# Two loads on ScalarE's queue, PSUM banks that stay open, and an intermediate that moves into another tile

## The chip, the cores and the metric

The kernel runs on one core of a Trainium2 chip. The metric is the device time of one execution in microseconds (us); the median of several runs counts. The engines are called PE (TensorE, matmuls), DVE (VectorE), ACT (ScalarE), POOL (GpSimd) and SP (SyncE, which here only issues DMAs). SBUF is the on-chip working memory, PSUM the accumulator memory, of which the kernel uses eight banks of 128 x 512 fp32.

## The reference

Three layers in a row. First, attention with a window: 2 batches x 8 heads, 768 positions, head size 64; a query sees the 128 latest keys and 4 "sink" keys at the start. Then a dense layer with a smooth activation, then a mixture of four experts with ReLU:

```python
scores = np.where(is_sink | in_window, scale * q @ k.T, -1e9)
x = softmax(scores) @ v                  # 1536 tokens x 512
h = x @ w_in                             # 512 -> 2048, w_in and w_out in float64
x = (h * np.tanh(softplus(h))) @ w_out   # "mish", 2048 -> 512
p = domain_probs / (domain_probs.sum(-1, keepdims=True) + 1e-09)
out = sum(p[:, e:e + 1] * (np.maximum(x @ w1[e], 0) @ w2[e]) for e in range(4))  # 512 -> 1024 -> 512
```

## The kernel before, in words

Every big product is made of three matmuls on split numbers: each operand is a high part (`xh`, `wih`, `gh`) and a low part (`xl`, `wil`, `gl`), and high x high, low x high and high x low are added in PSUM.

Attention is cut into 24 *items* of 256 queries and two heads (`attention_item`). An item's data is one `qk` tile (`load_item`, L129 to L135) and one `v` tile (`attention_values`, L204 to L212); both DMAs are issued from SP's queue. Items are loaded two ahead (`AHEAD`). Items 0 and 1 have their `qk` loaded ahead of the program's branch on a flag; their `v`, and all of items 2 and 3, are loaded behind it. The scores go from PE into PSUM (`sc`, L231), DVE takes mask and row minimum (L234), ACT the exponential (L238), PE transposes (L264) and multiplies by `v` (L277), and ACT and DVE write the result as `xh` and `xl` (L184, L185).

The dense layer and the experts are cut into *units* of 512 hidden columns: units 0 to 3 are the dense layer, 4 to 11 the experts. A unit's weights come in pieces. In the dense layer each piece is float64 and is taken apart by ACT (L116) and DVE (L117 to L124). The pieces of unit 0 and, written back to DRAM ("parked"), of unit 1 and half of unit 2 are converted during attention.

`Experts.stream` gives the dense work in *steps*. Unit 0 is run in four chunks of tokens, here A (0 to 255), B (256 to 511), C (512 to 1023) and D (1024 to 1535). A chunk has four hidden blocks (`layer1`: 12 matmuls into one `h` bank, then `mish`) and four output blocks (`layer2`: 12 matmuls into one `o` bank, from the `gh` and `gl` of all four hidden blocks). The order is: block 1, block 2, output 1 of the chunk before, block 3, output 2, block 4, outputs 3 and 4. While attention runs, one step follows each item from the sixth item on, 19 steps in all: all of A and B's hidden blocks, A's outputs, all four blocks of C and B's outputs 1 to 3. What comes behind is traced after the attention's pools are closed.

PSUM during attention: one `h` bank and one `o` bank, three for `sc`, two for the transposes, one for `pv`. Behind attention these pools are closed, and new ones are opened: two banks for the intermediate `r`, three for `h`, three for `o`. During attention `r` is one SBUF tile instead. `mish` (L549 to L556, then the split at L89 and L97) has five ACT instructions on tiles `w`, `u`, `r`, three on DVE, then ACT writes `gh` and POOL writes `gl`. `w` and `u` have two buffers, `gh` and `gl` seven.

The order of instructions on each engine is set when the program is built: the framework's planner takes the written order, moves an instruction forward where by its modelled times it is ready, and adds the semaphore waits. On the chip each engine then runs its queue strictly in that order.

Of the kernel before, what the change touches and what calls it, by code (L numbers as in the profile page):

```python
# [9 lines left out]
F32 = mybir.dt.float32  # L10
# [3 lines left out]
AF = mybir.ActivationFunctionType  # L14
ALU = mybir.AluOpType
PSUM = bass.MemoryType.PSUM

P = 128
BIG = 8.0e9
C2, C1, C0 = 0.4889076793633006, -0.9463237919407588, -0.8989585617169157  # L20
# [5 lines left out]
QW = 2 * P  # L26
# [99 lines left out]
        nc.sync.dma_start(out=park, in_=lo.bitcast(F32))  # L126


def load_item(c, b, hp, i, pool=None):  # L129

    w = c.KW[min(i, 1)]
    raw = c.stage.next() if pool is None else pool.tile([P, QW + c.KW[1]], F32, tag="qk", name="qk")
    off = c.OFF[i]
    c.nc.sync.dma_start(out=raw[:, 0:QW + w], in_=c.qk[b, hp, :, off:off + QW + w])
    return raw  # L135


# [63 lines left out]
    return a  # L201


def attention_values(c, a, b, hp, i):  # L204

    v = a.v.next()
    n0 = 0 if i else 1
    c.nc.sync.dma_start(
        out=v[:, n0:3],
        in_=c.v[b, hp, (2 * i - 1 + n0) * P:(2 * i + 2) * P, :].rearrange("(n p) d -> p n d", p=P),  # L210
    )
    return v  # L212
# [165 lines left out]
class Experts:  # L378
# [5 lines left out]
    def __init__(self, c, ctx):  # L384
        self.c = c
        self.NF = self.FU // P
        self.KT = c.DM // P
        tp = c.tc.tile_pool
        self.acc = c.acc
        self.wpool = [ctx.enter_context(tp(name="m_w0", bufs=1)), None]  # L390
        self.cv = ctx.enter_context(tp(name="m_cv", bufs=1))
        self.tp = ctx.enter_context(tp(name="m_t", bufs=2))
        self.gp = ctx.enter_context(tp(name="m_g", bufs=7))
        self.units = []
        for u in range(c.F1 // self.FU):
            cols = slice(2 * u * self.FU, 2 * (u + 1) * self.FU)
            self.units.append((0, u, c.w_in[:, cols], c.w_out[u * self.FU:(u + 1) * self.FU, :]))
        self.n1 = len(self.units)
        for e in range(c.E):
            for u in range(c.F2 // self.FU):  # L400
                cols = slice(u * self.FU, (u + 1) * self.FU)
                self.units.append((1, e, c.w1[e, :, cols], c.w2[e, cols, :]))
        self.w = {}
        self.parked = {}

    def psum(self, ctx, nh, no, nr=0):
        tp = self.c.tc.tile_pool
        self.pr = ctx.enter_context(tp(name="m_pr", bufs=nr or 1, **(dict(space=PSUM) if nr else {})))
        self.pa = ctx.enter_context(tp(name="m_pa", bufs=nh, space=PSUM))
        self.pb = ctx.enter_context(tp(name="m_pb", bufs=no, space=PSUM))  # L410

    def park(self, pool, n, nm):

# [51 lines left out]
    def layer1(self, n, t0, cw, g):  # L465
        c, nc = self.c, self.c.nc
        kind, e, _, _ = self.units[n]
        NF, KT, n1 = self.NF, self.KT, self.n1
        x = (c.xh, c.xl)
        cols = slice(t0, t0 + cw)  # L470
        wis = self.w[n][0]
        for f in range(NF):
            h = self.pa.tile([P, self.CW], F32, tag="h", name="h")[:, 0:cw]
            fs = slice(f * P, (f + 1) * P)
            for k in range(KT):
                for t, (sw, sx) in enumerate(TERMS):
                    nc.tensor.matmul(  # L477
                        h, lhsT=wis[sw][:, k, fs], rhs=x[sx][:, k, cols],
                        start=k == 0 and t == 0, stop=k == KT - 1 and t == 2,
                    )  # L480
            gh = self.gp.tile([P, self.CW], F32R, tag="gh", name="gh")[:, 0:cw]
            gl = self.gp.tile([P, self.CW], F32R, tag="gl", name="gl")[:, 0:cw]
            if kind == 0:
                self.mish(n, gh, gl, h)
            else:
                nc.scalar.activation(gh, h, AF.Relu)  # L486
                nc.vector.scalar_tensor_tensor(gl, h, 0.0, gh.bitcast(F32), ALU.max, ALU.subtract)  # L487
            g.append((gh, gl))
            yield

    def layer2(self, n, t0, cw, g):
        c, nc = self.c, self.c.nc
        kind, e, _, _ = self.units[n]
        NF, KT, n1 = self.NF, self.KT, self.n1
        cols = slice(t0, t0 + cw)
        wos = self.w[n][1]
        if kind == 0:
            accv = self.acc.rearrange("p (ch d) w -> p ch d w", d=KT)
            for d in range(KT):
                o = self.pb.tile([P, cw], F32, tag="o", name="o")  # L500
                ds = slice(d * P, (d + 1) * P)
                for f in range(NF):
                    for t, (sw, sx) in enumerate(TERMS):
                        nc.tensor.matmul(  # L504
                            o, lhsT=wos[sw][:, f, ds], rhs=g[f][sx],
                            start=f == 0 and t == 0, stop=f == NF - 1 and t == 2,
                        )
                y = accv[:, t0 // c.DM, d, t0 % c.DM:t0 % c.DM + cw]
                if n == 0:
                    nc.scalar.activation(y, o, AF.Copy)  # L510
                else:
                    nc.vector.tensor_tensor(y, y, o, ALU.add)
                if n == n1 - 1:
                    split(c, c.xh[:, d, cols], c.xl[:, d, cols], y, nc.scalar, nc.vector)
                yield
            return
        last = n == len(self.units) - 1
        for d in range(cw // P):
            tt = t0 // P + d
            pcol = c.pn[:, tt, e:e + 1]  # L520
            ds = slice(d * P, (d + 1) * P)
            nw = 2 if last and tt == c.T // P - 1 else 1
            for q in range(nw):
                ms = slice(q * c.DM // nw, (q + 1) * c.DM // nw)
                o = self.pb.tile([P, c.DM], F32, tag="o", name="o")[:, ms]
                for f in range(NF):
                    for t, (sw, sx) in enumerate(TERMS):
                        nc.tensor.matmul(  # L528
                            o, lhsT=g[f][sx][:, ds], rhs=wos[sw][:, f, ms],
                            start=f == 0 and t == 0, stop=f == NF - 1 and t == 2,  # L530
                        )
                y = self.acc[:, tt, ms]
                if n == n1:
                    nc.scalar.activation(y, o, AF.Copy, scale=pcol)
                else:
                    nc.vector.scalar_tensor_tensor(y, o, pcol, y, ALU.mult, ALU.add)  # L536
                if last:
                    nc.sync.dma_start(out=c.out[tt * P:(tt + 1) * P, ms], in_=y)
            yield

    def mish(self, n, gh, gl, h):

        c, nc = self.c, self.c.nc
        cw = h.shape[-1]
        w, u = (self.tp.tile([P, self.CW], F32, tag=t, name=t)[:, 0:cw] for t in ("w", "u"))
        r = self.pr.tile([P, self.CW], F32, tag="r", name="r")[:, 0:cw]
        nc.scalar.activation(w, h, AF.Tanh, scale=0.5)  # L549
        nc.scalar.activation(w, w, AF.Square, scale=-0.5, bias=0.5)  # L550
        nc.scalar.activation(u, w, AF.Square, scale=C2, bias=C1)
        nc.scalar.activation(r, u, AF.Exp, bias=C0)  # L552
        nc.vector.scalar_tensor_tensor(u, w, 1.0, r, ALU.add, ALU.mult)  # L553
        nc.scalar.activation(u, u, AF.Square, scale=ROOT2, bias=-1.5 * ROOT2)
        nc.vector.scalar_tensor_tensor(u, u, 1.5, r, ALU.add, ALU.mult)
        nc.vector.scalar_tensor_tensor(w, u, 1.0, h, ALU.subtract, ALU.mult)  # L556
        split(c, gh, gl, w, nc.scalar, nc.gpsimd)
# [10 lines left out]
def banded(c, ctx, raws):  # L568
# [3 lines left out]
    first = ExitStack()  # L572
    x = Experts(c, ctx)
    w = x.weights(0)
    x.psum(first, 1, 1)
    a = attention_pools(c, first)
    steps = x.stream([(0, 0, QW), (0, QW, QW)] + [(0, t0, x.CW) for t0 in range(2 * QW, c.T, x.CW)] + later(c, x, 1))
    dram = ctx.enter_context(tc.tile_pool(name="park", bufs=1, space=bass.MemoryType.DRAM))
# [1 line left out]
    items = c.items  # L580
    raws = dict(enumerate(raws))
    preps = {}
    done = 0
    for m, it in enumerate(items):
        while done <= min(m + AHEAD, len(items) - 1):
            raw = raws.pop(done) if done in raws else load_item(c, *items[done], pool=a.qk)
            preps[done] = raw, attention_values(c, a, *items[done])
            done += 1
        attention_item(c, a, *it, preps.pop(m))
        if m < 4 or m in PARK:  # L590
            run(w, 1)
        if m >= LAG:
            run(steps, 1)
        if m == 0:
            normalize_probs(c)
    first.close()
    x.wpool[1] = ctx.enter_context(tc.tile_pool(name="m_w1", bufs=1))
    x.psum(ctx, 3, 3, 2)
    run(x.weights(1))
    run(steps, 4 * (x.NF + 4) - 4 - (len(items) - LAG))  # L600
    rest(c, x, steps, 1)
# [140 lines left out]
```

## Time and profile before

| what | before |
| --- | --- |
| median of 3 runs | 935.59 us (931.53, 935.59, 936.59) |
| the profiled execution: its own time | 931.33 us |
| span of its instructions | 929.5 us |
| PE busy | 905.6 us, 97% of the span |
| DVE, ACT, POOL busy | 424.6, 347.7, 263.7 us |
| mean granted clock of PE | 0.988 of full speed |

The busy times are sums over the span. The profile's page also cuts the span into 40 slices; there DVE is at 9 tenths in slices 2 to 6 and at 1 or 2 tenths in the second half. A "row" below is a line of an answer of the trace: start in us, duration, engine, line of the kernel, operation, and in brackets how long the engine sat idle before and what ended that.

### The profile page before, as it was taken

How to read it: one execution, taken by the hardware profiler on the slowest of the kernel's cores; microseconds unless marked ns; L12 is line 12 of the kernel's file. 1: busy time of each engine (PE TensorE's matmuls, PEld its weight loads, DVE VectorE, ACT ScalarE, POOL GpSimd, SP SyncE). 2: the span in 40 equal slices, each digit the busy share in tenths (PEclk: the TensorE clock that was granted, in tenths of full speed). 3: DMA queues.
4: the chain of work that ended last, by engine and by line, in shares of the span. 5: the costliest groups of instructions: out<-in, count | busy, mean ns of one | idle time of the engine just before them, and what ended most of it. 6: DMA issues, size and time to landing. Idle time of an engine off the chain costs nothing.

```text
span 929.5 us, 11138 instructions
## 1 busy us (share of the span) xinstructions
PE 905.6 (97%) x4292; PEld 730.6 (79%) x4292; DVE 424.6 (46%) x770; ACT 347.7 (37%) x745; POOL 263.7 (28%) x217
## 2 busy tenths in 40 slices
PE   6999999799999999999999999999999999999997
PEld 4566767688888888888888888888888888888886
DVE  6999995247698555641112222222222222222222
ACT  4788875487767767722221111111111111111110
POOL 4586663122222434520220220221122112200000
PEclk8999999989999999999999999999999999999999
DMA  7757752062123011001110110110110010000012
GB/s 234 249 189 242 251 215 80 17 255 91 46 90 136 1 46 46 23 23 46 46 40 7 45 46 1 46 46 0 46 46 24 23 45 1 1 1 1 11 46 83
DMA packets 33790, 67.03 MB, mean 72 GB/s; under 512 B 4144, under 2 KB 12592, under 8 KB 33728
## 3 DMA queue, kind: packets, MB, share of 16 engines
q1 hardware_dynamic: 33728, 66.23, 21.1%
q8 instruction: 36, 0.59, 0.3%
q14 instruction: 26, 0.21, 0.1%
HBM read 51.54 MB, written 9.44 MB: 66 GB/s over the span
## 4 chain that ended last, share of the span: by engine, by line
PE 86%; DVE 10%; ACT 1%; DMA 1%; issue 0%; POOL 0%; DVEq 0%; ACTq 0%
PE h L477 42%; PE o L528 28%; PE o L504 14%; DVE pr L234 2%; DVE cv_h L119 1%; DVE cv_a L123 1%; PE pv L277 1%; DVE cv_a L117 1%; DVE cv_r L122 1%; DMA stage<-in_moe_w_in_dram 1%; PE sc L231 1%; PE tp L264 1%; DVE cv_a L121 1%; DVE xl L185 1%; DVE cv_a L118 0%
## 5 line engine op out<-in xcount | busy, mean ns | idle before, releaser
L477 PE MATMUL h<-xh,wih 128*128 128x512 f32 (+1 forms) x592 | 229.2, 387 | 0.3 <-DVE w L556 0.3
L477 PE MATMUL h<-xh,wil 128*128 128x512 f32 (+1 forms) x592 | 227.8, 385 | 0.0
L477 PE MATMUL h<-xl,wih 128*128 128x512 f32 (+1 forms) x592 | 226.8, 385 | 0.0
L486 ACT ACTIVATE gh<-h 128x512 fp32r<-128x512 f32 x96 | 57.4, 598 | 410.1 <-PE h L477 245.2
L487 DVE SCALAR_TENSOR_TENSOR gl<-h,gh 128x512 fp32r<-128x512 f32 x96 | 66.4, 691 | 208.1 <-ACT gh L486 207.9
L528 PE MATMUL o<-wol,gh 128*128 128x512 f32 (+1 forms) x388 | 150.1, 387 | 0.0
L528 PE MATMUL o<-woh,gh 128*128 128x512 f32 (+1 forms) x388 | 150.1, 387 | 0.0
L528 PE MATMUL o<-woh,gl 128*128 128x512 f32 (+1 forms) x388 | 149.9, 387 | 0.0
L536 DVE SCALAR_TENSOR_TENSOR acc<-o,pn,acc 128x512 f32<-128x512 f32 (+1 forms) x85 | 63.3, 745 | 176.2 <-PE o L528 176.2
L477 PEld LDWEIGHTS h<-xh,wih 128*128 128x128 f32 x592 | 111.8, 189 | 24.5 <-DVE cv_a L117 0.7
L477 PEld LDWEIGHTS h<-xl,wih 128*128 128x128 f32 x592 | 111.5, 189 | 22.6 <-issue 0.5
L477 PEld LDWEIGHTS h<-xh,wil 128*128 128x128 f32 x592 | 111.7, 189 | 22.3 <-DVE wil L124 0.3
L97 POOL TENSOR_TENSOR gl<-w,gh 128x512 fp32r<-128x512 f32 (+1 forms) x52 | 68.2, 1312 | 168.0 <-ACT gh L89 167.8
L504 PE MATMUL o<-gh,woh 128*128 128x512 f32 (+1 forms) x208 | 79.4, 382 | 5.4 <-ACT gh L89 5.4
L528 PEld LDWEIGHTS o<-wol,gh 128*128 128x128 f32 x388 | 72.9, 188 | 14.9
L528 PEld LDWEIGHTS o<-woh,gh 128*128 128x128 f32 x388 | 72.9, 188 | 14.9
L528 PEld LDWEIGHTS o<-woh,gl 128*128 128x128 f32 x388 | 72.8, 188 | 14.7
L504 PE MATMUL o<-gh,wol 128*128 128x512 f32 (+1 forms) x208 | 78.2, 376 | 0.0
L504 PE MATMUL o<-gl,woh 128*128 128x512 f32 (+1 forms) x208 | 77.4, 379 | 0.0
L87 POOL TENSOR_SCALAR wih<-stage 128x1024 fp32r<-128x1024 f32 x16 | 16.5, 1048 | 189.4 <-PE h L477 189.4
L553 DVE SCALAR_TENSOR_TENSOR u<-w,r 128x512 f32<-128x512 f32 (+1 forms) x52 | 34.4, 662 | 50.2 <-ACT r L552 49.9
L87 POOL TENSOR_SCALAR woh<-stage 128x1024 fp32r<-128x1024 f32 x16 | 16.5, 1048 | 141.0 <-PE o L528 122.2
(84 smaller groups left out, 1101.5 us busy)
## 6 DMA issues: line engine op xcount, KB each, us to landing
stage<-in_moe_w_dram SPq DMA_DIRECT2D x32, 512.0 KB, 3.7
stage<-in_moe_w_in_dram SPq DMA_DIRECT2D x8, 1024.0 KB, 6.6
stage<-in_moe_w_out_dram SPq DMA_DIRECT2D x8, 1024.0 KB, 5.0
qk<-in_qk_dram SPq DMA_DIRECT2D x16, 324.0 KB, 5.4
acc<-in_v_dram SPq DMA_DIRECT2D x16, 192.0 KB, 3.6
woh<-cv_h SPq DMA_DIRECT2D x6, 512.0 KB, 2.9
out_dram<-acc SPq DMA_DIRECT2D x11, 256.0 KB, 2.0
wih<-cv_h SPq DMA_DIRECT2D x4, 512.0 KB, 3.0
```

The source lines that it names most:

```text
L87: eng.tensor_scalar(out, src, 1.0, 0.0, ALU.mult, ALU.add)
L97: eng_lo.tensor_tensor(lo, src, hi.bitcast(F32), ALU.subtract)
L117: nc.vector.tensor_scalar(af, af, TINY_HI, HUGE_HI, ALU.max, ALU.min)
L119: nc.vector.scalar_tensor_tensor(h, w_hi, -0x40000000, a, ALU.bitwise_and, ALU.bitwise_or)
L234: nc.vector.tensor_tensor_reduce(out=o, in0=sc, in1=c.masks[t if i == 0 else 2][:, 0:sw], scale=-c.scale, scalar=3.0e38, op0=ALU.add, op1= ...
L477: nc.tensor.matmul(h, lhsT=wis[sw][:, k, fs], rhs=x[sx][:, k, cols], start=k == 0 and t == 0, stop=k == KT - 1 and t == 2,)
L486: nc.scalar.activation(gh, h, AF.Relu)
L487: nc.vector.scalar_tensor_tensor(gl, h, 0.0, gh.bitcast(F32), ALU.max, ALU.subtract)
L504: nc.tensor.matmul(o, lhsT=wos[sw][:, f, ds], rhs=g[f][sx], start=f == 0 and t == 0, stop=f == NF - 1 and t == 2,)
L528: nc.tensor.matmul(o, lhsT=g[f][sx][:, ds], rhs=wos[sw][:, f, ms], start=f == 0 and t == 0, stop=f == NF - 1 and t == 2,)
L536: nc.vector.scalar_tensor_tensor(y, o, pcol, y, ALU.mult, ALU.add)
L553: nc.vector.scalar_tensor_tensor(u, w, 1.0, r, ALU.add, ALU.mult)
```

## The change

Three edits. (1) The `qk` and `v` loads of items 2 and 3 are issued from ACT's queue instead of SP's. (2) The `h` bank and the `o` bank of the attention stage are no longer closed with it; behind attention two more of each are opened and taken in rotation with the old one, instead of three new ones of each. (3) In the attention stage the intermediate `r` of `mish` is written into the `gl` tile of the same block, whose final content overwrites it at the end; the SBUF tile for it is gone.

```diff
-def load_item(c, b, hp, i, pool=None):
+def load_item(c, b, hp, i, pool=None, eng=None):
-    c.nc.sync.dma_start(out=raw[:, 0:QW + w], in_=c.qk[b, hp, :, off:off + QW + w])
+    (eng or c.nc.sync).dma_start(out=raw[:, 0:QW + w], in_=c.qk[b, hp, :, off:off + QW + w])
...
-def attention_values(c, a, b, hp, i):
+def attention_values(c, a, b, hp, i, eng=None):
-    c.nc.sync.dma_start(
+    (eng or c.nc.sync).dma_start(
...
     def psum(self, ctx, nh, no, nr=0):
         tp = self.c.tc.tile_pool
-        self.pr = ctx.enter_context(tp(name="m_pr", bufs=nr or 1, **(dict(space=PSUM) if nr else {})))
-        self.pa = ctx.enter_context(tp(name="m_pa", bufs=nh, space=PSUM))
-        self.pb = ctx.enter_context(tp(name="m_pb", bufs=no, space=PSUM))
+        k = len(self.banks)
+        if nr:
+            self.pr = ctx.enter_context(tp(name="m_pr", bufs=nr, space=PSUM))
+        for nm, n in (("h", nh), ("o", no)):
+            pool = ctx.enter_context(tp(name=f"m_p{nm}{k}", bufs=n, space=PSUM))
+            self.banks.setdefault(nm, []).extend([pool] * n)
+
+    def bank(self, nm):
+        pools = self.banks[nm]
+        pools.append(pools.pop(0))
+        return pools[-1].tile([P, self.CW], F32, tag=nm, name=nm)
...
-            h = self.pa.tile([P, self.CW], F32, tag="h", name="h")[:, 0:cw]
+            h = self.bank("h")[:, 0:cw]
...
-        r = self.pr.tile([P, self.CW], F32, tag="r", name="r")[:, 0:cw]
+        rr, r = gl, gl.bitcast(F32)
+        if self.pr:
+            rr = r = self.pr.tile([P, self.CW], F32, tag="r", name="r")[:, 0:cw]
-        nc.scalar.activation(r, u, AF.Exp, bias=C0)
+        nc.scalar.activation(rr, u, AF.Exp, bias=C0)
...
-    x.psum(first, 1, 1)
+    x.psum(ctx, 1, 1)
...
-            raw = raws.pop(done) if done in raws else load_item(c, *items[done], pool=a.qk)
-            preps[done] = raw, attention_values(c, a, *items[done])
+            eng = c.nc.scalar if done in (2, 3) else None
+            raw = raws.pop(done) if done in raws else load_item(c, *items[done], pool=a.qk, eng=eng)
+            preps[done] = raw, attention_values(c, a, *items[done], eng=eng)
...
-    x.psum(ctx, 3, 3, 2)
+    x.psum(ctx, 2, 2, 2)
```

The three places that took an `o` tile take `self.bank("o")` in the same way.

## Rows read from the trace of the kernel before

**Rows 1.** Page, head: busy us of each engine.

```profile
PE 905.6 (97%) x4292; PEld 730.6 (79%) x4292; DVE 424.6 (46%) x770; ACT 347.7 (37%) x745; POOL 263.7 (28%) x217
```

**Rows 2.** Stages: start:end, length, busy us (count) by engine, granted clock, DMA share, GB/s.

```profile
12.00:18.00 6.00, 2.75 (x14) 1.73 (x13) 2.46 (x12) 2.80 (x8) 2.85 (x5) 0.91 1.00 341
16.30:136.00 119.70, 112.75 (x734) 76.22 (x734) 116.76 (x308) 96.89 (x301) 78.18 (x82) 0.96 0.70 237
136.00:178.60 42.60, 42.50 (x241) 33.79 (x242) 18.80 (x34) 21.99 (x51) 12.03 (x11) 0.96 0.17 62
178.60:184.78 6.18, 0.83 (x4) 0.37 (x3) 2.07 (x3) 3.87 (x8) 0.00 (x0) 0.95 0.03 6
184.78:191.00 6.22, 6.22 (x15) 4.87 (x16) 2.64 (x4) 5.40 (x11) 2.57 (x2) 0.50 0.97 317
191.00:922.00 731.00, 731.00 (x3228) 605.31 (x3227) 273.58 (x380) 214.48 (x360) 163.14 (x103) 1.00 0.12 42
```

**Rows 3.** Timeline of the start: PE, ACT and DVE.

```profile
8.81 0.40 ACT L238 ACTIVATE pr<-pr,mx 128x128 f32<-128x128 f32 x1 [6.80 <-DVE mx L234]
...
16.30 1.12 ACT L116 ACTIVATE cv_a<-stage 128x1024 f32<-128x1024 f32 x1 [2.87 <-DMA stage<-in_moe_w_in_dram]
17.15 0.77 PE L231 MATMUL sc<-qk 64*128 64x128 f32 x2 [3.17 <-DMA qk<-in_qk_dram]
...
17.45 0.69 DVE L117 TENSOR_SCALAR cv_a<-cv_a 128x1024 f32<-128x1024 f32 x1 [2.62 <-ACT cv_a L116]
...
18.06 0.42 DVE L234 CUSTOM_DVE_ANT_0 pr<-sc,mask 128x256 f32<-128x256 f32 x1
...
20.48 0.28 DVE L234 CUSTOM_DVE_ANT_0 pr<-sc,mask 128x128 f32<-128x128 f32 x1
...
21.96 0.61 DVE L252 TENSOR_SCALAR pr<-pr,sm 128x128 f32<-128x128 f32 x2
```

**Rows 4.** Timeline of SP's DMA issues at the start.

```profile
8.20 0.39 SPq L134 DMA_DIRECT2D qk<-in_qk_dram  x1
8.70 0.37 SPq L208 DMA_DIRECT2D acc<-in_v_dram  x1
9.18 0.40 SPq L372 DMA_DIRECT2D stage<-in_moe_w_in_dram  x1
9.69 0.40 SPq L134 DMA_DIRECT2D qk<-in_qk_dram  x1
```

**Rows 5.** DMA issues of 0 to 30 us: count, KB each, median us to landing.

```profile
stage<-in_moe_w_in_dram SPq DMA_DIRECT2D x2, 1024.0 KB, 8.0
...
acc<-in_v_dram SPq DMA_DIRECT2D x4, 128.0 KB, 2.1
qk<-in_qk_dram SPq DMA_DIRECT2D x2, 256.0 KB, 5.2
```

**Rows 6.** Chain that ended last: start us, us, what (the load; then 163 to 200 us).

```profile
9.18 7.10 DMA stage<-in_moe_w_in_dram
...
163.41 4.98 PE h L477 x21
...
184.78 4.21 PE o L504 x9
...
196.84 2.72 PE h L477 x12
```

**Rows 7.** Timeline of ACT, DVE and PE behind attention.

```profile
162.84 0.69 DVE L556 SCALAR_TENSOR_TENSOR w<-u,h 128x512 f32<-128x512 f32 x1
...
177.49 1.09 ACT L549 ACTIVATE w<-h 128x512 f32<-128x512 f32 x2 [2.49 <-PE h L477]
...
179.50 1.15 ACT L551 ACTIVATE u<-w 128x512 f32<-128x512 f32 x2
...
183.38 0.69 DVE L556 SCALAR_TENSOR_TENSOR w<-u,h 128x512 f32<-128x512 f32 x1
...
184.63 0.58 ACT L552 ACTIVATE r<-u 128x512 f32<-128x512 f32 x1
184.78 0.79 PE L504 MATMUL o<-gh,woh 128*128 128x512 f32 x1 [5.35 <-ACT gh L89]
...
190.81 0.60 ACT L549 ACTIVATE w<-h 128x512 f32<-128x512 f32 x1
```

**Rows 8.** Waits of SP's own DMA queue, longest in total: us, times, longest.

```profile
SPq L434 <- DVE u L555: 35.2, 1, 35.2
```

More of the change, by code (lines that the diff above doesn't have):

```diff
@@ L403, in __init__ @@
         self.w = {}
+        self.banks, self.pr = {}, None
         self.parked = {}
@@ L499, in layer2 @@
             for d in range(KT):
-                o = self.pb.tile([P, cw], F32, tag="o", name="o")
+                o = self.bank("o")[:, 0:cw]
                 ds = slice(d * P, (d + 1) * P)
@@ L524, in layer2 @@
                 ms = slice(q * c.DM // nw, (q + 1) * c.DM // nw)
-                o = self.pb.tile([P, c.DM], F32, tag="o", name="o")[:, ms]
+                o = self.bank("o")[:, ms]
                 for f in range(NF):
```

## The prediction

> **What bounds the kernel now.** I read the engines' busy times first: PE works 905.6 us of the span and no other engine half of it [rows 1]. Then the stages [rows 2]. From 191 to 922 us PE is busy in all 731 us at full clock; the change adds and removes no matmul, so nothing is to be had there. From 16.3 to 136 us DVE is busy for 116.76 of 119.7 us: this stage ends when DVE has done its attention and weight conversions. From 136 to 178.6 PE has 42.50 of 42.60. What is left is three places: the start, up to 16.3 us; a hole in PE behind attention (178.6 to 184.78); and what follows that hole, 6.22 us at a granted clock of 0.50, which is the lower level, 1.2 GHz, after 5.35 us in which PE had nothing. Only 15 matmuls fit there; at full clock 12 take 2.72 us [rows 6], so 15 would take 3.40, and the low clock costs 2.8 us. Hole and low clock together are 8.2 us.
>
> At the start two things wait for DMAs [rows 3]: PE for the `qk` of item 3 (3.17 us, until 17.15), and ACT, with DVE behind it, for the first piece of `w_in` (until 16.30; DVE then starts at 17.45 after 2.62 us of nothing). SP's issues show why: the 1024 KB piece goes out at 9.18, item 3's `qk` behind it at 9.69 [rows 4, 5], and the piece takes 7.10 us [rows 6].
>
> In the hole, PE waits for ACT's `gh` of chunk C's block 4. All four blocks of C are traced inside attention, with its single `h` bank. So block 3 can only start when block 2's last reader (162.84 + 0.69 = 163.53) is done, block 4 when block 3's is, and the `gh` of block 4 comes at 184.7 [rows 7]. PE fills the time with blocks 1, 2 and 3 of chunk D, which have three fresh banks, until it has nothing left.
>
> **Part by part. (1) The loads.** Four issues leave SP (two `qk`, two `v`). SP's stand 0.5 us apart [rows 4], so the piece of `w_in` can go out at 8.20 instead of 9.18, 1.0 us sooner. On ACT no DMA issue appears in the trace; by SP's the four cost 4 x 0.5 = 2.0 us. ACT has nothing before 8.81 (6.80 us idle) [rows 3], so they run from about 7.2 to 9.2 and delay the first exponential by at most 0.4 us, which is hidden as long as DVE waits for `w_in` until 17.45. If the planner puts two of them between exponentials, it is 1.0 us and still inside that cover.
>
> Items 2 and 3 then travel beside the piece, not ahead of and behind it. Its end is pushed back by item 3's 256 + 128 KB; at the 341 GB/s of this stretch [rows 2] that is 1.15 us, against the 1.0 us of earlier issue. So the piece lands between 1.0 us sooner and 1.2 us later; I take 0.5 later. In exchange DVE can fill its 2.62 us hole: two 256-wide mask steps (0.42 each), two 128-wide (0.28) and a scaling pair (0.61) now stand behind L117 [rows 3], 2.0 us in all. So the start gains 2.0 - 0.5 = 1.5 us. Best: 2.0 + 1.0 = 3.0. Worst: the planner leaves that work behind L117 and the piece is late, a loss of 1.2. DVE has 3 us of slack in the next 120 us [rows 2], so I pass the 1.5 us on whole.
>
> The Trainium skill ("DMA: Bandwidth & Descriptors", section "Rules for kernel authors") speaks against this edit: spreading DMAs over several issuing engines adds no bandwidth, because they share the same 16 DMA engines and interleave, and only issue time is saved. The trace agrees that the DMA engines are full there (share 1.00 from 12 to 18 us); by that rule alone this part is worth zero or a small loss, which is the second rival.
>
> **(2) The banks.** Behind attention the rotation for `h` begins with the old bank. Chunk D's block 1 therefore gets the bank that block 4 of C holds until 183.38 + 0.69 = 184.07. Its 12 matmuls, which before were filler ahead of the hole, move behind it: 2.72 us of cover are lost. Two things come back. These 12 can start at 184.07, not at 184.78 with the `gh`: 0.71 us. And the filler had stood in the way: between 163.41 and 168.39 PE did 21 matmuls [rows 6], of which only 12 were block 3 of C; without D's block 1, blocks 3 and 4 of C come 0.7 us (3 of those 21) to 2.0 us (all 9) sooner; I take 1.3. Sum: 2.72 - 0.71 - 1.3 = 0.7 us lost. Best: the chain of C runs early enough to close the hole, 8.2 us gained. Worst: nothing sooner, and the 12 run wholly at the low clock (12 x 6.22 / 15 = 4.98), 4.98 - 0.71 = 4.3 lost. I stay at 0.7, since the single bank for C's four blocks, which makes the hole, is left as it is.
>
> The two PSUM banks of `r` no longer lie on the old `h` and `o` banks. Before, D's block 1 stood from 180.65 (end of L551) to 184.63 for one [rows 7]. That stall goes; it buys nothing on PE, which never waits again after 184.78. `o` has three banks before and after.
>
> **(3) `r` in `gl`.** ACT writes and DVE reads as many elements in SBUF as before, so the twelve blocks in question cost the same. `gl` is held from the exponential on, about 4 us longer, of seven buffers; since C's blocks wait for the `h` bank anyway, the seventh is not what comes last. Zero; at most one 0.6 us instruction either way. With the SBUF tile gone, the loads of unit 1's weights needn't wait 35.2 us for its last reader at 183.3 [rows 8]. They move into a stretch where the DMA share is 0.17 and later 0.03, off 184.78 to 191, where it is 0.97 [rows 2]. PE had no wait for them, so this is zero too.
>
> **Sum.** -1.5 + 0.7 = -0.8 us: the profiled execution would go from 931.33 to 930.5. The median of the runs lies 4.26 us above that execution, so on its scale it is 935.59 - 0.8 = 934.8 us. Such a step is less than a measurement of this kernel can tell: about 0.5%, 4.7 us.
>
> **Rivals.** *The hole closes* (faster). If the planner, with the stalls on `r` gone and fewer fillers at hand, puts C's blocks ahead of D's, the hole and the low clock behind it go: -8.2 - 1.5 = -9.7, 925.9 us. For it: block 3 stood 2.0 us behind foreign matmuls, and blocks 2 to 4 follow each other. Against: two full passes of `mish` at 6.6 us (177.49 to 184.07) stay in the chain, and half a hole may bring the low clock all the same.
>
> *The loads share the DMA engines* (no gain at the start): the piece lands 1.2 us later, DVE sits before L117 for that time, and the items gained early wait behind it in the queue. +1.2 + 0.7 = +1.9, 937.5 us. For it: DMA share 1.00. Against: DVE has ready work.
>
> *The kept bank starts a second hole* (slower). D's block 1 is done at 184.07 + 4.98 = 189.05, and its `mish` ends with the bank at 195.6 (6.6 later). PE's store from 184.07 on is 12 of block 1, 9 parts of C's outputs [rows 6] and C's output 4 (12): 33 matmuls, 15 in 6.22 and 18 in 4.08 us, to 194.4. Then 1.2 us of waiting for a bank. D's block 3 can take `w` and `u` only from block 1; before, they were held from the pair's second Tanh, at about 178.0, to 190.81 less the 4.0 of stall, 8.8 us, so its bank is free at 189.05 + 8.8 + 6.6 = 204.5, a second wait of about 1.1 us. If PE then drops to the low clock again, 2.8 more. 2.7 - 0.7 + 1.2 + 1.1 + 2.8 = +7.1, less the 1.5 of the start: +5.6, 941.2 us. It decides if D's blocks 2 and 3 do not get through `mish` while block 1 waits for its bank. For it: only two pairs of `w` and `u`. Against: both blocks are complete early and ACT is idle for over a third of 178.6 to 184.78 [rows 2].
>
> **How the numbers follow.** Forecast 0.56 (934.8; by itself 931 to 939, from the bounds of its terms short of the extremes); hole closed 0.17 (925.9, faster); shared DMAs 0.12 (937.5, no change); second hole 0.15 (941.2, slower in four cases of five). Tails of the forecast give each side 0.03 more. Faster 0.20, within the 4.7 us 0.65, slower 0.15. The range of 8 in 10 goes halfway into the two outer cases: 925.5 to 941.5.
>
> **What would show it.** Right: PE's wait for item 3 gone; an early mask step ahead of L117; the first ACT conversion between 15.3 and 17.5; still a hole of 4 to 8 us behind attention that ends on `gh`, at a `gh` one or two us sooner, then a stretch at 0.50; unit 1's weight loads well ahead of 183; from then on PE without a gap. Wrong: no low clock near 185 (hole closed), the first conversion later than 17.5 with DVE waiting (shared DMAs), PE waits for an `h` bank around 194 and 204 (second hole), or a stage that I cost at nothing, 16 to 136 us, with another length.

## The result and the profile after

The changed kernel takes 948.92 us (median of four runs, 947.92 to 951.8), the kernel before 936.09 on the same chip (four runs, 931.53 to 939.42): a ratio of 1.0145, 95% interval 1.0097 to 1.0194. It is slower; I had forecast 934.8 and a range that ended at 941.5. The profiled execution took 951.8 us with a span of 950.0 at a mean granted clock of 0.972; before it was 931.33, 929.5 and 0.988. Of these 20.5 us the medians confirm 12.8: executions of the kernel before lie in two groups, 929.3 to 934.5 us at a mean clock of 0.978 to 0.991 and 935.5 to 939.6 at 0.975 to 0.983, and its profile is from the faster one. So amounts are taken from medians, and the traces show places.

The head of the page, busy us of each engine, answers [rows 1]:

```profile
PE 918.3 (97%) x4292; PEld 739.5 (78%) x4292; DVE 424.4 (45%) x770; ACT 350.7 (37%) x745; POOL 261.0 (27%) x217
```

PE runs the same 4292 instructions and is busy 12.7 us longer: that is clock. The other 20.5 - 12.7 = 7.8 us is PE idle. Both have their places in the stages, which answer [rows 2] (start:end, length, busy us and count by engine, granted clock, DMA share, GB/s):

```profile
12.00:18.00 6.00, 2.25 (x14) 1.28 (x12) 1.79 (x11) 2.06 (x6) 2.76 (x4) 0.90 1.02 377
16.30:136.00 119.70, 112.72 (x669) 76.21 (x670) 107.55 (x288) 91.80 (x282) 69.64 (x76) 0.86 0.65 219
136.00:178.60 42.60, 40.57 (x252) 31.15 (x251) 25.63 (x49) 24.41 (x61) 16.42 (x17) 0.92 0.40 138
178.60:213.00 34.40, 23.37 (x84) 17.80 (x83) 7.91 (x12) 16.01 (x28) 3.48 (x3) 0.88 0.20 82
213.00:922.00 709.00, 709.00 (x3126) 587.19 (x3125) 267.38 (x369) 212.04 (x355) 163.75 (x104) 1.00 0.12 38
```

From 213 us on PE is busy in every microsecond at full clock, as it was from 191 before. The loss lies ahead of that, in two places. From 16.3 to 136 us PE is busy as long as before but does 669 instructions instead of 734, at 0.86 instead of 0.96, and DVE, which was busy for 116.76, has 107.55: it now waits. The last item of attention ends its work (`xl`) at 173.2 instead of 164.3; part of these 8.9 us belongs to the execution that was profiled, since in a run below with PE's order of before it comes at 171.2. And behind attention there is not one hole of 5.35 us but four, as PE's waits from 160 to 215 us show (us in total, times, longest):

```profile
PE h L488 <- DVE w L570: 10.3, 3, 3.6
PE o L515 <- ACT acc L521: 0.7, 1, 0.7
```

**The start**: SP's issues, answering [rows 4], then the timeline of ACT's issues, PE, ACT and DVE, answering [rows 3].

```profile
8.22 0.40 SPq L372 DMA_DIRECT2D stage<-in_moe_w_in_dram  x1
```

```profile
6.85 0.38 ACTq L134 DMA_DIRECT2D qk<-in_qk_dram  x1
...
9.01 0.35 ACTq L134 DMA_DIRECT2D qk<-in_qk_dram  x1
...
9.74 0.39 ACTq L208 DMA_DIRECT2D acc<-in_v_dram  x1
...
16.14 0.46 PE L231 MATMUL sc<-qk 64*128 64x128 f32 x2 [2.35 <-DMA qk<-in_qk_dram]
...
16.78 1.12 ACT L116 ACTIVATE cv_a<-stage 128x1024 f32<-128x1024 f32 x1 [3.67 <-DMA stage<-in_moe_w_in_dram]
...
17.93 0.69 DVE L117 TENSOR_SCALAR cv_a<-cv_a 128x1024 f32<-128x1024 f32 x1 [3.64 <-ACT cv_a L116]
18.54 0.42 DVE L234 CUSTOM_DVE_ANT_0 pr<-sc,mask 128x256 f32<-128x256 f32 x1
```

The piece of `w_in` goes out 0.96 us sooner and arrives 0.48 later: the 0.5 that I took. Item 3's `qk` comes 1.01 us sooner. But DVE's mask step for it stands behind L117 in the queue, so DVE's hole grew from 2.62 to 3.64 us. One execution does not fix these amounts: with the same four loads, in the first run below, the conversion starts at 15.52, which is 0.78 sooner than before.

**Inside attention** two stretches show what happens later: 46 to 62 and 142 to 160 us, of after, then of before.

```profile
46.00:62.00 16.00, 14.79 (x66) 10.11 (x66) 10.88 (x31) 9.95 (x28) 10.97 (x12) 0.57 0.38 116
142.00:160.00 18.00, 15.97 (x91) 11.67 (x90) 15.63 (x26) 10.89 (x29) 9.96 (x10) 0.81 0.35 123
```

```profile
46.00:62.00 16.00, 15.13 (x99) 9.77 (x98) 15.96 (x42) 13.90 (x45) 14.31 (x15) 1.00 0.61 199
142.00:160.00 18.00, 18.00 (x117) 14.60 (x116) 8.30 (x10) 9.05 (x20) 5.17 (x5) 1.00 0.18 59
```

In these stretches lie gaps of PE of 1.21 and 1.98 us; behind them the clock falls, to 0.57 and 0.81 over the stretch, and in the first DVE in turn waits for PE (timeline of PE and DVE, after):

```profile
48.08 1.11 PE L264 MATMUL tp<-ident,pr 128*128 128x128 f32 x4 [1.21 <-POOL pr L255]
...
55.98 0.43 DVE L234 CUSTOM_DVE_ANT_0 pr<-sc,mask 128x260 f32<-128x260 f32 x1 [2.82 <-PE sc L231]
...
61.54 0.43 DVE L234 CUSTOM_DVE_ANT_0 pr<-sc,mask 128x260 f32<-128x260 f32 x1 [2.29 <-PE sc L231]
...
149.00 1.11 PE L277 MATMUL pv<-pt,acc 128*64 128x256 f32 x12 [1.98 <-DVE xl L185]
```

**Behind attention** (timelines of PE and ACT, answering [rows 7]; L563 is the Tanh, L549 before):

```profile
182.49 0.60 ACT L563 ACTIVATE w<-h 128x512 f32<-128x512 f32 x1 [7.02 <-PE h L488]
188.03 0.80 PE L488 MATMUL h<-xh,wih 128*128 128x512 f32 x1 [3.61 <-DVE w L570]
192.47 0.60 ACT L563 ACTIVATE w<-h 128x512 f32<-128x512 f32 x1 [3.82 <-PE h L488]
198.01 0.80 PE L488 MATMUL h<-xh,wih 128*128 128x512 f32 x1 [3.60 <-DVE w L570]
202.57 1.09 ACT L563 ACTIVATE w<-h 128x512 f32<-128x512 f32 x2 [3.95 <-PE h L488]
205.24 0.50 PE L515 MATMUL o<-gh,woh 128*128 128x512 f32 x1 [0.70 <-ACT acc L521]
211.38 0.79 PE L488 MATMUL h<-xh,wih 128*128 128x512 f32 x1 [3.12 <-DVE w L570]
```

C's block 3 ends its matmuls; its `mish` holds the old bank from the Tanh at 182.49 to 188.03, 5.54 us; then block 4 is computed, and its `mish` again holds the bank for 5.54 us, until 198.01; then D's block 1, and its `mish` releases the bank at 211.38, for D's block 4. One bank serves four blocks in a row, and each time PE has only some outputs to do meanwhile. D's blocks 1 and 2 have their Tanh together at 202.57: block 2 had not got through `mish` while block 1 waited. That is the condition under which the rival of the second hole was to decide, with the two pairs of `w` and `u` as its reason.

### The profile page after: what moved, and what is told of

Its sections match the earlier page's. It is cut to its first block, busy times and chain, and to the rows that moved or that the text cites. A ratio compares the mean times of both kernels' runs of the same rounds, so it can differ in the third digit from the quotient of the medians.

```text
span 950.0 us, 11139 instructions
## 1 busy us (share of the span) xinstructions
PE 918.3 (97%) x4292; PEld 739.5 (78%) x4292; DVE 424.4 (45%) x770; ACT 350.7 (37%) x745; POOL 261.0 (27%) x217
## 4 chain that ended last, share of the span: by engine, by line
PE 89%; DVE 5%; POOL 1%; ACT 1%; DMA 1%; issue 1%; ACTq 0%; POOLq 0%; DVEq 0%
PE h L488 42%; PE o L539 28%; PE o L515 13%; PE sc L231 2%; PE pv L277 2%; PE tp L264 1%; DVE pr L234 1%; POOL pr L255 1%; DMA stage<-in_moe_w_in_dram 1%; PE pv L283 1%; DVE cv_a L123 1%; DVE cv_h L119 0%; DVE cv_r L122 0%; DVE cv_l L124 0%; DVE cv_a L121 0%
## 5 line engine op out<-in xcount | busy, mean ns | idle before, releaser
L488 PE MATMUL h<-xh,wih 128*128 128x512 f32 (+1 forms) x592 | 232.7, 393 | 10.3 <-DVE w L570 10.3
L488 PE MATMUL h<-xh,wil 128*128 128x512 f32 (+1 forms) x592 | 230.6, 389 | 0.0
L488 PE MATMUL h<-xl,wih 128*128 128x512 f32 (+1 forms) x592 | 230.5, 389 | 0.0
L488 PEld LDWEIGHTS h<-xh,wih 128*128 128x128 f32 x592 | 113.9, 192 | 37.1 <-DVE w L570 11.6
L488 PEld LDWEIGHTS h<-xl,wih 128*128 128x128 f32 x592 | 113.9, 192 | 22.9 <-DVE xl L185 0.3
L488 PEld LDWEIGHTS h<-xh,wil 128*128 128x128 f32 x592 | 114.2, 193 | 22.5 <-DVE wil L124 0.4
L539 PEld LDWEIGHTS o<-woh,gl 128*128 128x128 f32 x388 | 72.9, 188 | 14.8
L539 PEld LDWEIGHTS o<-wol,gh 128*128 128x128 f32 x388 | 72.9, 188 | 14.8
L238 ACT ACTIVATE pr<-pr,mx 128x260 f32<-128x260 f32 (+2 forms) x96 | 46.5, 486 | 12.4 <-DVE mx L234 11.4
```

The lines of the kernel that those rows point to most:

```text
L238: nc.scalar.activation(o, o, AF.Exp, bias=mx[:, e:e + 1], scale=-1.0, accum_out=sm[:, e:e + 1])
L488: nc.tensor.matmul(h, lhsT=wis[sw][:, k, fs], rhs=x[sx][:, k, cols], start=k == 0 and t == 0, stop=k == KT - 1 and t == 2,)
L539: nc.tensor.matmul(o, lhsT=g[f][sx][:, ds], rhs=wos[sw][:, f, ms], start=f == 0 and t == 0, stop=f == NF - 1 and t == 2,)
```

## The experiments

**Each edit alone.** The load edits as in the diff, without the bank edits:

> The kernel before with edit 1 alone (items 2 and 3 loaded from ACT's queue). Theory: this edit is the cause of the 8.9 us that the attention stage lost (last xl at 173.2 instead of 164.3), because the planner's order of POOL and PE work changes and PE falls to 1.2 GHz after idle gaps of over 1 us in the stage 46 to 92 us. Then the last xl comes at 172 to 174 us, the hole behind attention stays one hole of about 5 us ended by gh, and the time is 8 to 10 us over before (about 945). Rival A: edit 2 or 3 slowed attention (the h bank or gl held longer): then the last xl stays within 1.5 us of 164.3 and the time within 2 us of before.

939.38 us against 934.29: 1.0059 (1.0031 to 1.0087). Slower, by 5 us where I had expected 8 to 10, with the last `xl` at 171.7 and the one hole behind attention as before (5.35 us, on `gh`). PE's waits from 16 to 160 us gained one of 1.4 for a mask step, a `pv` wait of 1.6 and the 1.2 for POOL seen in after. But behind this last one, which ends at 47.47, the clock stays full (46 to 62 us at 1.00, where after has 0.57).

The bank edits alone (`r` stays an SBUF tile):

```diff
-    x.psum(first, 1, 1)
+    x.psum(ctx, 1, 1)
+    x.pr = first.enter_context(tc.tile_pool(name="m_pr", bufs=1))
...
-    x.psum(ctx, 3, 3, 2)
+    x.psum(ctx, 2, 2, 2)
```

> The kernel before with edit 2 alone (h and o banks kept open, two new ones of each; r stays in its SBUF tile during attention; loads on SP). Theory: attention is as before (last xl at 163 to 166 us), but behind it PE waits three times for an h bank (3 to 4 us each, low clock after each), so the time is 9 to 12 us over before (about 946). Rival: the second and third hole of the changed kernel come only from the late attention; then there is one hole as before, and the time is within 3 us of before.

944.53 against 934.29: 1.0097 (1.0065 to 1.0129). PE's waits, 160 to 215 us:

```profile
PE h L488 <- DVE w L570: 10.0, 3, 3.6
PE o L515 <- ACT acc L521: 0.7, 1, 0.7
```

Attention is even 4.9 us earlier here (last `xl` at 159.4), and the holes are the same as in after: they belong to this edit, and a late attention is not their cause.

`r` in `gl` alone:

```diff
-        r = self.pr.tile([P, self.CW], F32, tag="r", name="r")[:, 0:cw]
+        rr, r = gl, gl.bitcast(F32)
...
-        nc.scalar.activation(r, u, AF.Exp, bias=C0)
+        nc.scalar.activation(rr, u, AF.Exp, bias=C0)
```

> The kernel before with edit 3 alone (r in gl while attention runs). Theory: nothing, within 2 us of before; unit 1's weight loads leave the wait for the last reader of r and start some 10 us earlier or more. Rival: gl held from the exponential on is what makes block 4 of a chunk late; then the h bank's waits appear here too and the time is 3 us or more over before.

933.97 against 934.29: 0.9993 (0.9964 to 1.0023). Nothing, as forecast. Banks and `r` together, loads as before:

> The changed kernel with the loads of items 2 and 3 back on SP's queue (edits 2 and 3). Theory: as e2_banks within 2 us (about 946 or 9 to 12 us over before); the last xl at 163 to 166 us. Rival A (edit 2 or 3 slows attention): the last xl at 172 to 174 and the time as the changed kernel's.

944.02: 1.0106 (1.0057 to 1.0155), as the banks alone. So 5.1 us for the loads, 9.7 for banks and `r`: 14.8, where the whole change measured 12.8.

**Which load.** Item 2's two loads alone on ACT's queue (`if done == 2`), then item 3's alone (`if done == 3`):

> The kernel before with only item 2's two loads on ACT's queue; item 3 stays on SP. The planner then gives every engine the order of before; only the queue of two DMAs differs. Theory: what edit 1 costs comes from the new order of the engines' work in the attention stage, not from the transfers, so this is within 2 us of before. Rival: it comes from the transfers (first piece of w_in later, DVE's conversions later); then half of edit 1's 5 us, 2 to 4 us over before, and the first conversion on ACT later than 16.5 us.

> The kernel before with only item 3's two loads on ACT's queue. Here the planner does change the order of PE, DVE and POOL in the attention stage (about 1200 lines of PE's list, as many as with all four loads). Theory (order): 3 to 6 us over before, with PE gaps of over 1 us between 40 and 150 us and stretches at the lower clock behind them. Rival (transfers): as with item 2 alone, or less than 2 us.

Item 2: 933.01 against 937.01, 0.9943 (0.9923 to 0.9964, five runs), with the engines' order of before. Item 3: 939.10, 1.0026 (1.0009 to 1.0044), with another order: its last `xl` comes at 175.1. That order is not the one of the changed kernel either. On this chip the slowest execution with item 2 (935.26) lies below the fastest with item 3 (937.16), although in both traces the first conversion starts sooner than before, at 15.46 and 15.54. The cost comes with item 3, and is less than the 3 to 6 us that I expected. Two runs were meant to separate the queue from the order. In the first, item 2's loads and item 3's `qk` go to ACT's queue, item 3's `v` stays on SP, and the planner keeps the order of before; in the second all loads stay on SP, but item 3 is loaded one item sooner, and PE, DVE and POOL get the order of the run with item 3 alone, line for line:

```diff
# first
-            preps[done] = raw, attention_values(c, a, *items[done])
+            preps[done] = raw, attention_values(c, a, *items[done], eng=eng if done == 2 else None)
# second
-        while done <= min(m + AHEAD, len(items) - 1):
+        while done <= min(max(m + AHEAD, 3), len(items) - 1):
```

> The kernel before with item 2's two loads and item 3's qk on ACT's queue; only item 3's v stays on SP. The planner gives PE, DVE and POOL the order of before. Theory (order): no cost; 0 to 6 us under before, as e5_item2_act. Rival (transfers): with both qk beside the first piece of w_in, that piece is late as in the changed kernel (ACT's first conversion at 16.6 us or later) and the time is 2 to 5 us over before.

> The kernel before with all loads on SP's queue, but item 3 loaded one item earlier. The planner gives PE, DVE and POOL the order that they have in e6_item3_act, line for line. Theory (order): the same loss as e6_item3_act or more, 2 to 7 us over before, although no load is on ACT. Rival (transfers): within 1.5 us of before.

Order kept: 936.63 against 935.63, 1.0024 (0.9989 to 1.0058): neither the gain that I expected nor a clear loss. New order without ACT's queue: 941.19, 1.0065 (1.0038 to 1.0092). Of ten runs each on one chip, the slowest of the first (939.23) lies below the fastest of the second (939.53). So a price of this kind is there without a single issue from ACT. But the second run moves a transfer as well: item 3's loads stand ahead of the piece of `w_in` in SP's queue, which goes out at 10.22 instead of 9.18 (its timelines of SP, ACT and PE):

```profile
10.22 0.40 SPq L372 DMA_DIRECT2D stage<-in_moe_w_in_dram  x1
...
18.49 1.12 ACT L116 ACTIVATE cv_a<-stage 128x1024 f32<-128x1024 f32 x1 [3.22 <-DMA stage<-in_moe_w_in_dram]
...
20.73 1.22 PE L231 MATMUL sc<-qk 64*128 64x256 f32 x2 [3.86 <-DVE mx L234]
```

The first conversion starts at 18.49; it was 16.30 before and 15.40 with the order kept. So the 0.65% is not the order's alone. Its windows show the stretches of after in part:

```profile
16.30:46.00 29.70, 25.84 (x103) 14.50 (x101) 22.18 (x62) 17.22 (x51) 12.04 (x15) 0.66 0.69 239
46.00:62.00 16.00, 16.00 (x107) 9.87 (x107) 15.41 (x48) 14.18 (x48) 11.90 (x13) 1.00 0.66 208
142.00:160.00 18.00, 15.14 (x82) 11.23 (x80) 14.95 (x23) 9.78 (x24) 7.66 (x7) 0.81 0.42 152
```

The low clock from 46 to 62 us is not there, and the other two are no mark of a new order, since the run with the order kept has 0.71 and 0.81 in them. Two things do go with a new order. PE waits once for 1.6 to 2.1 us for `xl` ahead of a `pv` product, between 141 and 149 us, in all three runs with a new order and in after; with PE's order of before the longest such wait is 0.9. And of the 28 executions of those three runs none took less than 937.16 us, while 46 of 112 of the kernel before, 4 of 5 with item 2 alone and 3 of 10 with the order kept took less than 935.

**Which bank first.** The bank edits alone, with the new banks put ahead of the old one in the rotation:

```diff
-            self.banks.setdefault(nm, []).extend([pool] * n)
+            self.banks[nm] = [pool] * n + self.banks.get(nm, [])
```

> Edit 2 alone as in e2_banks, but the rotation of h and o banks behind attention starts with the two new banks; the old one comes third. One edit against e2_banks. Theory: e2_banks loses because chunk D's block 1, first in the rotation, waits for block 4 of C, and blocks 2 and 3 of D wait in turn for the w and u pairs that block 1 takes ahead of them. With the new banks first, D's blocks 1 and 2 get through mish early, the holes at 182 and 194 us go, and the time falls from e2_banks' +10 to +1 to +4 over before. Rival: the loss is only that PE has two banks of filler instead of three; then the order of the banks changes nothing and it stays at +8 to +11.

940.11 against 937.01: 1.0028 (1.0004 to 1.0051) instead of 1.0097. Two holes are left of four:

```profile
PE h L488 <- DVE w L570: 7.3, 2, 5.1
```

The same one line in the whole changed kernel:

> The changed kernel with one edit: behind attention the rotation of banks starts with the new banks. Theory: 6 us under the changed kernel, which is 5 to 9 us over before; what is left is edit 1's. Rival: in the whole change the late attention hides the difference; then within 2 us of the changed kernel (12 us or more over before).

944.09 against 935.63: 1.0088 (1.0064 to 1.0113) instead of 1.0145. The start of the rotation is 5 to 6 us of the cost in either kernel.

**Can the hole be closed?** In the kernel before, the last two of the 19 steps that were traced between the items are traced behind attention's end, where the three banks are (`BACK = 2`):

```diff
-        if m >= LAG:
+        if LAG <= m < len(items) - BACK:
...
-    run(steps, 4 * (x.NF + 4) - 4 - (len(items) - LAG))
+    run(steps, 4 * (x.NF + 4) - 4 - (len(items) - LAG - BACK))
```

> The kernel before, with the last two of the 19 dense steps traced behind the close of attention's pools instead of inside it: chunk C's block 4 and output 2 of B. Block 4 then gets a fresh h bank and needn't wait for block 3's mish. Theory: the hole of before (5.35 us) and the 2.8 us at the lower clock behind it come from C's four blocks on one bank; they go, and the time is 5 to 8 us under before. Rival: the hole is the length of mish itself, whatever bank; then a hole of 3 us or more stays behind attention and the time is within 3 us of before.

936.93 against 937.01: 0.9995 (0.9967 to 1.0022). The hole is 4.0 us instead of 5.35, still on `gh`: that is the rival, and a fresh bank for block 4 does not close it. Next, the change with the pieces that cost least (item 2 alone on ACT, new banks first), and on top of it, with `r` in `gl` throughout, more `h` banks as filler: 3, 4 and 5 new ones.

```diff
-    x.psum(ctx, 2, 2, 2)
+    x.psum(ctx, 3, 3, 0)   # then 4, 2, 0 and 5, 1, 0
```

> The changed kernel with two edits: only item 2 is loaded from ACT's queue, and the rotation behind attention starts with the new banks. Theory: edit 1 costs by the order that item 3's load brings, edit 2 by the old bank coming first; both are mended, so the time falls from 1.0145 of before to within 3 us of it (e5_item2_act gained 5 us, e7_new_banks_first lost 3). Rival: the costs don't add up like this, because the planner's order changes again: then 5 us or more over before.

> As e9_mended, but r lies in gl to the end of unit 3, so PSUM's two r banks are free: one old and three new banks for h, the same for o, new ones first. Chunk D's blocks 1 to 3 then have fresh banks as in the kernel before. Theory (filler): with 36 matmuls of filler again, one hole of 4 to 6 us ended by gh, and no other; 2 to 6 us under before, since item 2's load gains. Rival: gl held from the exponential on (seven buffers) delays each chunk's block 4, PE waits for gl or gh in the stretch 200 to 400 us, and it is slower than before.

> As e10_h3_o3, with four new banks for h and two for o. Chunk D's block 4 has a fresh bank too: 48 matmuls of filler, 2.72 us more. Theory (filler): the hole is 2 to 3 us; the time 2 to 4 us under e10_h3_o3's. Rival: the hole is set by mish and keeps its length, because what fills it is taken from work that is done ahead anyway: no difference to e10_h3_o3 beyond 1.5 us.

> As e10_h3_o3, with five new banks for h and one for o: room for unit 1's first block as well, whose weights no longer wait for r's SBUF tile. Theory (filler): 60 matmuls, the hole is under 1 us or gone, and with it the lower clock behind it; but o has only two banks, so gaps of under 1 us at outputs may come in the steady stage. Time 4 to 9 us under before. Rival: with two o banks PE waits for every evacuation (0.6 us on ACT) and the steady stage from 200 us on is longer by 10 us or more.

The first took 938.93 against 936.31: 1.0016 (0.9989 to 1.0042). The others 0.9996, 0.9990 and 0.9998, each with an interval of some 0.3% to either side; the gains that I expected did not come. PE's waits for a bank in these three, from 160 to 215 us:

```profile
PE h L488 <- DVE w L570: 4.4, 1, 4.4
```

```profile
PE h L488 <- DVE w L570: 5.1, 1, 5.1
```

```profile
PE h L488 <- DVE w L570: 5.8, 1, 5.8
```

More filler does not close the hole: it is done ahead of C's block 4, whose Tanh comes at 184.4, 185.3 and 187.4. My theory that the hole lacks filler fell here. The series of `mish` passes through one bank is long, but 4.0 us of the hole stayed when block 4 had a bank of its own, so what sets its length is not settled.

**A version that beats both?** Order kept, `r` in `gl`, banks as before:

> e13_order_kept with edit 3 (r in gl while attention runs), and without edit 2: the parts of the change that the runs found harmless or useful. PE's order is that of before. Theory: costs and gains add, 3 to 6 us under before. Rival: edit 3 changes DVE's and ACT's order so that the gain is lost: within 2 us of before.

934.37 against 935.63: 0.9990 (0.9965 to 1.0014). It beats the changed kernel, not the one before. The 0.6% of item 2 alone did not come again in the six later kernels that contain it (0.9990 to 1.0024), so I don't claim it.

## Why the prediction was wrong

**The start, "a gain of 1.5 us that passes on whole".** The time of the piece was right in the profiled execution (0.5 late) and wrong in that of the load edits alone (0.78 sooner), so the hit is in part luck. The use of DVE's hole was wrong: the ready work stayed behind L117, which I had kept as the worst case. The rival of the shared DMA engines describes the profiled start better, with 0.48 us for its 1.2.

**The stage from 16 to 136 us, "costed at nothing".** This is the first step that failed. I took DVE as the bound with 3 us of slack, and its order as given. But the planner writes the order of every engine anew when item 3 is ready sooner. In the profile after, PE is without work for 1.21 us at 48, 1.31 at 81 and 1.98 at 149; behind each the clock falls, and PE becomes what DVE waits for. Measured: +5 us where I had -1.5. ACT's queue is not needed for a loss, as the run on SP shows. For the order speak the 28 executions without one under 937.16 us, and item 3 alone against item 2 alone on one chip. The size is open: item 3 alone cost 0.26%, the run on SP, with that same order, 0.65% and a late piece, and neither has the changed kernel's own order. Which of the moved instructions opens PE's gaps is not settled, nor why the 1.21 us gap comes with a low clock in after and not in the load edits' own trace.

**The banks, "+0.7".** The second failed step, in the size of a term whose mechanism I had priced as a rival: the kept bank starts a second hole. I let the old bank block D's block 1 once, at 184, and took the lost filler off once. In fact PE's queue had C's block 4 next, without D's block 1 as filler ahead of it, so the wait for the bank between blocks 3 and 4 of C, hidden before, became a hole as well. The rival's +7.1 for this part is near the 6.9 us between the spans of the bank edits' execution (936.4, at 0.987) and the one before (929.5, at 0.988); the medians give 9 to 10. That nearness is in part luck: the rival kept the hole on `gh` and added waits of 1.2 and 1.1 us, and the trace has 3.6, 3.3, 3.1 and 0.7 us in place of the 5.35. What I held against it (D's blocks 2 and 3 are complete early, ACT is idle) did not count, as their `w` and `u` come in turn behind block 1's: in after their matmuls have ended by 178.3, and block 2's Tanh comes at 202.57. "C's blocks 0.7 to 2.0 us sooner" did not happen either: the Tanhs of C's blocks 3 and 4 came at 168.49 and 177.49 before, and at 169.20 and 180.33 with the bank edits.

**`r` in `gl` and unit 1's loads, zero.** Right: no difference alone, and the first of those loads went out at 171.90 with no wait of PE on it before or after.

## What to carry to other kernels

An edit that only makes data ready sooner is a new input to whatever orders the instructions: compare the two orders before costing the stage at nothing. When a buffer with a reader still to come joins a rotation, put it last, and count every block that it serves in a row, not only the first. An engine with little slack that bounds a stage stays the bound only as long as the clock of the engine beside it does.

## What I had not expected of the hardware

With PE's order of before, the granted clock still differs from trace to trace. From 16.3 to 46 us it was 0.89 in the profile before, 0.71 in the run with the order kept and 0.66 in the last kernel above, whose spans are 929.5, 935.1 and 931.0 us. So this stretch alone does not set the time: from 142 to 160 us the three have 1.00, 0.81 and 1.00. I take from it that a gain or loss of half a per cent needs ten runs or more on either side here. And a PE gap of 1.21 us stands ahead of a 16 us stretch at a mean of 0.57, 6.9 us of full clock, though PE was busy for 14.79 of it. The gap's length alone does not tell: the same gap in the load edits' own trace was followed by full clock, and before, a gap of 1.05 us ahead of 31.21 was followed by full clock (28 to 38 us at 1.00), one of 0.89 ahead of 62.95 by 0.79 (62 to 70 us).
